# Weight conversion in bits, a batch turned by TensorE, and another order of pieces, in a linear-attention and mixer kernel

## The chip, the cores and the metric

The kernel runs on one core of a Trainium2 chip. The metric is the device time of one execution in microseconds (us). A profile of one execution gives, for every instruction, its engine, start and length; its span runs from the first to the last instruction.

## The reference

Inputs are `q`, `k`, `v`, `f_logit` of shape (4, 8, 768, 48) in float32, and the float64 weights `U` (768 x 32), `V` (32 x 768), `w_ch1` (384 x 1536) and `w_ch2` (1536 x 384).

```python
f = 1.0 / (1.0 + np.exp(-f_logit))
for t in range(S):
    state = f[:, :, t, :, None] * state + np.einsum('bhd,bhe->bhde', k[:, :, t], v[:, :, t])
    y[:, :, t] = np.einsum('bhd,bhde->bhe', q[:, :, t], state)
x = y.transpose(0, 2, 1, 3).reshape(B, S, H * D)
u = x + (x.transpose(0, 2, 1) @ U @ V).transpose(0, 2, 1)
out = u + np.maximum(u @ w_ch1, 0.0) @ w_ch2
```

## The kernel before

A unit is two heads of one batch (16 units, four a batch), with 2 x 48 head dimensions padded to 2 x 64 partitions and the 768 steps in six chunks of 128.

`prepare(n)` readies a unit. SyncE has loaded f, k and q into `f_raw`, `k_raw`, `q_raw` (two sets) so that VectorE can turn them (dimension to partition) by one transpose of 32 x 32 blocks each (`turned`, L237). `gates` makes the sigmoid on ScalarE (L255, L257), `keep` a backward scan X on VectorE (L261) with four small instructions, `keys` turns k, which GpSimd multiplies by X (L276), `read` is the forward scan Y (L280), `queries` turns q, which GpSimd multiplies by Y (L285), and issues the loads of unit n + 2.

`attend(n)` uses it: `scores` (two halves) multiplies k and q on TensorE (`sc`, L308) and VectorE masks the result (`A`, L315); `kept` turns k back on TensorE (`pt`, L327), copied by ScalarE (`kb`, L329); `states` makes the state changes (`ds`, L335) and adds them up on VectorE (`st`, L341, L346); `read` makes the outputs (`y`, L363 and L372), copied by ScalarE into the batch's `x` (L378).

The mixer of a batch is a list of pieces: `low_rank` (`ph`, L79, copied to `h`), six `mix` (`pu`, L86; VectorE adds it to x, L87), six `turn` (`put`, L95; copied to `uT`, L97), then for each half of the tokens twelve `ch1` (`pz`, L102; ScalarE's ReLU gives `z`, L105) and three `ch2` (`po`, L111; VectorE adds x, L114, SyncE stores). The pieces of the mixer of batch b are strewn in equal numbers among the pieces of the units of batch b + 1 by `fill`; the last mixer follows at the end.

The weights come in 32 pieces, strewn in the same way among batch 0's units. `load` fetches a piece into `w_raw` (two buffers; `V` takes four loads a piece) and converts float64 to float32 by six VectorE instructions (L49, L51, L53 to L56) and two GpSimd ones (L57, L58).

All loads and stores are issued by SyncE, in one order. A scheduler of the framework sorts the instructions into one fixed order for each engine when the program is built, starting from the order in which they are written; on the chip each engine goes through its own in that order, waiting on semaphores. The PSUM pools hold three large buffers (`ps_big`: `sc`, `pt`, `y`) and two small ones (`ps_mm`: all else). A second path for the case that X gets too small is built, and skipped at run time.

Of the kernel before, what the change touches and what calls it, by code (L numbers as in the profile page):

```python
# [8 lines left out]
F32 = mybir.dt.float32  # L9
# [12 lines left out]


def weight_loader(nc, pool, one, dma):

    P = nc.NUM_PARTITIONS  # L30

    def load(dst, w, copies=1):
        rows, cols = dst.shape
        n = rows // copies
        if w.dtype == F32:
            for i in range(copies):
                dma.dma_start(out=dst[i * n : (i + 1) * n, :], in_=w)
            return
        raw = pool.tile([P, WP], U64, name="w_raw")
        for i in range(copies):  # L40
            dma.dma_start(out=raw[i * n : (i + 1) * n, 0:cols], in_=w)
        words = raw[0:rows, 0:cols].bitcast(U32).rearrange("p (n two) -> p n two", two=2)
        lo, hi = words[:, :, 0], words[:, :, 1]

        def tmp(dtype, name):
            return one.tile([P, WP], dtype, name=name)[0:rows, 0:cols]

        head, m = tmp(U32, "w_head"), tmp(F32, "w_m")
        nc.vector.tensor_scalar(head, hi, 0xFFFFF, 0x100000, ALU.bitwise_and, ALU.bitwise_or)  # L49

        nc.vector.scalar_tensor_tensor(m, lo, 2.0**-32, head, ALU.mult, ALU.add)  # L51
        e, e8, s = tmp(U32, "w_e"), tmp(U32, "w_e8"), tmp(U32, "w_s")
        nc.vector.tensor_scalar(e, hi, 20, 0x7FF, ALU.logical_shift_right, ALU.bitwise_and)  # L53
        nc.vector.tensor_scalar(e8, e, 1023.0 - 127.0, 0.0, ALU.subtract, ALU.max)
        nc.vector.tensor_scalar(e, e8, 255.0, 2.0**23, ALU.min, ALU.mult)
        nc.vector.scalar_tensor_tensor(s, hi, 0x80000000, e, ALU.bitwise_and, ALU.bitwise_or)  # L56
        nc.gpsimd.tensor_scalar(m, m, 2.0**-20, None, ALU.mult)  # L57
        nc.gpsimd.tensor_tensor(dst, m, s.bitcast(F32), ALU.mult)  # L58

    return load  # L60


def mixer_pieces(nc, b, x, U, V, w1, w2, ident, out, two, three, zp, ps_mm):

# [64 lines left out]
def factored_path(ctx, tc, q, k, v, f_logit, moe_U, moe_V, moe_w_ch1, moe_w_ch2, out, ok):  # L129
# [257 lines left out]
    for piece in prepare(0):  # L387
        piece()
# [364 lines left out]
```

## Time and profile before

| | |
|---|---|
| time before, median of 3 runs | 663.54 us (661.59 to 666.61) |
| the profiled execution | 667.96 us, its span 666.2 us |
| busy in the span | TensorE 544.8 (82%), VectorE 326.5 (49%), GpSimd 127.3 (19%), ScalarE 96.8 (15%) |
| moved by the DMA queues | 48.44 MB in 42,471 packets |

In a profile's rows PE is TensorE's matmuls (PEld its weight loads, which run beside them), DVE VectorE, ACT ScalarE, POOL GpSimd and SP SyncE. A float32 product of 128 x 128 by 128 x 384 is two MATMUL instructions in the trace, and one in the order. `x24` counts instructions.

### The profile page before, as it was taken

The page shows a single profiled execution, that of the slowest core. Times are in us where ns is not written, and L with a number is a line of the kernel's source. Part 1 is how long each engine was busy: PE and PEld are TensorE (multiplying, and loading weights), DVE is VectorE, ACT ScalarE, POOL GpSimd, SP SyncE. Part 2 cuts the span into 40 slices and gives each one's busy share as a digit, 9 for nine tenths or more (in the row PEclk, how much of TensorE's full clock was granted, in tenths as well). Part 3 has the DMA queues.
Part 4 walks back from the last instruction along what each step waited for, and adds up shares of the span by engine and source line. Part 5 has one row for each costly group of instructions (what it writes and reads, how often), then busy time and mean ns, then how long its engine had stood idle before and what let it go on. Part 6 is the DMA issues. An engine that isn't in the chain of part 4 may idle for free.

```text
span 666.2 us, 8766 instructions
## 1 busy us (share of the span) xinstructions
PE 544.8 (82%) x3593; PEld 339.3 (51%) x3593; DVE 326.5 (49%) x534; ACT 96.8 (15%) x189; POOL 127.3 (19%) x107
## 2 busy tenths in 40 slices
PE   0555037277099999999999999999999998999996
PEld 0554034054066565646655556566556564555553
DVE  5669799999985674365642652473011102000000
ACT  1100001012021032021220220212101201210200
POOL 2123464655642201202111111021100000000000
PEclk9999999999579999996999999979999999999999
DMA  9901654544589050295002522210000000000000
GB/s 203 187 1 36 146 142 115 138 116 130 145 181 209 31 120 0 64 201 119 5 19 76 141 66 63 74 25 1 1 24 14 0 13 26 0 1 35 0 14 28
DMA packets 42471, 48.44 MB, mean 73 GB/s; under 512 B 29878, under 2 KB 32950, under 8 KB 42422
## 3 DMA queue, kind: packets, MB, share of 16 engines
q1 hardware_dynamic: 42422, 47.79, 29.7%
q8 instruction: 30, 0.49, 0.3%
q14 instruction: 19, 0.16, 0.1%
HBM read 43.06 MB, written 4.72 MB: 72 GB/s over the span
## 4 chain that ended last, share of the span: by engine, by line
PE 67%; DVE 18%; DMA 7%; issue 3%; SPq 2%; POOL 1%; ACT 1%; DVEq 0%; POOLq 0%; ACTq 0%
PE po L111 27%; PE pz L102 27%; PE sc L308 4%; PE y L372 3%; DVE w_m L51 2%; DVE kT L237 2%; DMA q_raw<-in_q_dram 2%; PE pu L86 2%; DMA w_raw<-in_moe_w_ch_dram 2%; DMA k_raw<-in_k_dram 2%; DVE fT L237 2%; SPq L179 1%; DVE qT L237 1%; DVE w_head L49 1%; DVE X L261 1%
## 5 line engine op out<-in xcount | busy, mean ns | idle before, releaser
L102 PE MATMUL pz<-uT,w 128*128 128x384 f32 x576 | 202.5, 505 | 1.2 <-ACT z L105 1.2
L111 PE MATMUL po<-w,z 128*128 128x384 f32 x576 | 189.2, 488 | 0.0
L102 PEld LDWEIGHTS pz<-uT,w 128*128 128x128 f32 x576 | 110.0, 196 | 74.4 <-issue 6.3
L111 PEld LDWEIGHTS po<-w,z 128*128 128x128 f32 x576 | 108.7, 190 | 74.7
L308 PE MATMUL sc<-qT,kT 48*128 48x128 f32 x384 | 42.7, 356 | 92.2 <-POOL qT L285 92.2
L114 DVE TENSOR_TENSOR o<-x,po 128x384 f32<-128x384 f32 x24 | 13.3, 556 | 182.7 <-PE po L111 182.7
L308 PEld LDWEIGHTS sc<-qT,kT 48*128 48x128 f32 x384 | 34.2, 246 | 105.6 <-POOL qT L285 94.4
L105 ACT ACTIVATE z<-pz 128x384 f32<-128x384 f32 x96 | 47.0, 490 | 223.3 <-PE pz L102 223.3
L276 POOL TENSOR_TENSOR kT<-kT,X 128x768 f32<-128x768 f32 x16 | 29.4, 1836 | 239.8 <-DVE kT L237 166.2
L315 DVE TENSOR_TENSOR A<-sc,causal 128x384 f32<-128x384 f32 x64 | 33.2, 551 | 73.0 <-PE sc L308 72.9
L57 POOL TENSOR_SCALAR w_m<-w_m 128x384 f32<-128x384 f32 (+1 forms) x32 | 34.1, 1065 | 34.3 <-DVE w_m L51 25.6
L237 DVE STREAM_TRANSPOSE fT<-f_raw 128x768 f32<-128x768 f32 x16 | 33.3, 2079 | 9.8 <-DMA f_raw<-in_f_logit_dram 9.8
L285 POOL TENSOR_TENSOR qT<-qT,Y 128x768 f32<-128x768 f32 x16 | 29.2, 1827 | 45.9 <-DVE qT L237 40.4
L237 DVE STREAM_TRANSPOSE qT<-q_raw 128x768 f32<-128x768 f32 x16 | 33.6, 2099 | 6.6 <-PE y L363 6.6
L261 DVE TENSOR_TENSOR_SCAN X<-fz,ends 128x768 f32<-128x768 f32 x16 | 28.4, 1775 | 15.9 <-ACT f L257 10.9
L237 DVE STREAM_TRANSPOSE kT<-k_raw 128x768 f32<-128x768 f32 x16 | 33.1, 2071 | 0.0
L372 PE MATMUL y<-v_nat,A 128*64 128x48 f32 x768 | 32.1, 252 | 0.0
L363 PE MATMUL y<-st,qT 48*64 48x48 f32 x640 | 20.7, 255 | 13.6 <-DVE st L346 8.6
L280 DVE TENSOR_TENSOR_SCAN Y<-fz,starts 128x768 f32<-128x768 f32 x16 | 28.1, 1755 | 6.3 <-POOL qT L285 5.5
L372 PEld LDWEIGHTS y<-v_nat,A 128*64 128x64 f32 x768 | 29.9, 167 | 1.1
L86 PE MATMUL pu<-h,V 128*128 128x384 f32 x48 | 25.0, 622 | 6.1 <-ACT h L82 2.5
L58 POOL TENSOR_TENSOR w<-w_m,w_s 128x384 f32<-128x384 f32 x24 | 26.1, 1087 | 16.1 <-DVE w_s L56 16.0
(49 smaller groups left out, 320.2 us busy)
## 6 DMA issues: line engine op xcount, KB each, us to landing
w_raw<-in_moe_w_ch_dram SPq DMA_DIRECT2D x24, 384.0 KB, 3.8
f_raw<-in_f_logit_dram SPq DMA_DIRECT2D x63, 142.0 KB, 4.9
k_raw<-in_k_dram SPq DMA_DIRECT2D x63, 142.0 KB, 4.2
q_raw<-in_q_dram SPq DMA_DIRECT2D x63, 142.0 KB, 4.6
v_nat<-in_v_dram SPq DMA_DIRECT2D x32, 144.0 KB, 5.4
out_dram<-o SPq DMA_DIRECT2D x24, 192.0 KB, 1.9
w_raw<-in_moe_V_dram SPq DMA_DIRECT2D x8, 96.0 KB, 2.2
w_raw<-in_moe_U_dram SPq DMA_DIRECT2D x6, 32.0 KB, 1.8
```

The lines of the kernel that those rows point to most:

```text
L57: nc.gpsimd.tensor_scalar(m, m, 2.0**-20, None, ALU.mult)
L86: nc.tensor.matmul(pm[:, 0:DM], lhsT=V[:, t * P : (t + 1) * P], rhs=h[0], start=True, stop=True)
L102: nc.tensor.matmul(pm[:, 0:HALF], lhsT=w1[:, m, i * P : (i + 1) * P], rhs=uT[a][:, m, :], start=(m == 0), stop=(m == NDC - 1))
L105: nc.scalar.activation(z[a, i], pm[:, 0:HALF], AF.Relu)
L111: nc.tensor.matmul(pm[:, 0:DM], lhsT=z[a, i][:, s * P : (s + 1) * P], rhs=w2[:, i, :], start=(i == 0), stop=(i == NFC - 1))
L237: nc.vector.transpose(t.rearrange("p (i c) -> p c i", c=TB), bass.AP(src_tile.tensor, src_tile.offset, [list(src_tile.ap[0]), [D, TB], [1, ...
L261: nc.vector.tensor_tensor_scan(backwards(X, S - 1, S), backwards(f, S, S), backwards(ends, S - 1, S), 0.0, ALU.mult, ALU.add,)
L276: nc.gpsimd.tensor_tensor(kT, kT, T["X"], ALU.mult)
L285: nc.gpsimd.tensor_tensor(qT, qT, T["Y"], ALU.mult)
L308: nc.tensor.matmul(sc[:, par, c * C : (c + 1) * C], lhsT=T["k"][rows[par], chunk[g * G + c]], rhs=T["q"][rows[par], chunk[g * G + c]], sta ...
L315: nc.vector.tensor_tensor(T["A"][:, par, g * G : (g + 1) * G, :], sc[:, par, 0 : G * C].rearrange("p (c i) -> p c i", i=C), causal.unsquee ...
L372: nc.tensor.matmul(o(a, par, c), lhsT=T["A"][:, par, c, halves[a]], rhs=vt[:, c, par, :], start=False, stop=True, skip_group_check=True,)
```

## The change

1. A weight piece takes two ScalarE instructions (L57, L58), three VectorE ones (L59 to L61) and one integer addition on GpSimd (L62). `w_raw` has three buffers, and a piece's load is issued two pieces ahead of its conversion (`ahead_by`). `U` is one piece and each piece of `V` one load: 27 pieces.
2. f, k and q of batch 0 are loaded as they lie in memory, in runs of 192 bytes, turned by TensorE (`on_tensor`, six transposes each) and taken from PSUM by ScalarE: f by the sigmoid, k and q by a copy.
3. `w_ch2` is converted among the first pieces of the first mixer, in batch 1's units, no longer in batch 0's. `Fill` strews by a cost that each piece carries.
4. The pieces of a unit and of the next unit's preparation stand in another order, with `kept` ahead of the scores.
5. The three `ch2` of a mixer's second half stand after the next batch's attention, around `low_rank` and `mix` of the next mixer.
6. The sigmoid's table is loaded at the start.

TensorE's queue at the start. `sc`, `pt`, `ds` and `y` are as above; in the new order `pt` with `f_raw`, `k_raw`, `q_raw` are the six transposes of an operand. Before:

```order
L308 MATMUL sc<-qT,kT 128x128 x6
L327 MATMUL pt<-ident,kT 128x64 x10
L308 MATMUL sc<-qT,kT 128x128 x6
L335 MATMUL ds<-v_nat,kb 64x48 x10
L363 MATMUL y<-st,qT 64x48 x20
```

After:

```order
L321 MATMUL pt<-ident,f_raw_80 128x128 x6
L321 MATMUL pt<-ident,k_raw_81 128x128 x6
L321 MATMUL pt<-ident,q_raw_82 128x128 x6
L321 MATMUL pt<-ident,f_raw_83 128x128 x6
L418 MATMUL pt<-ident,kT 128x64 x10
L321 MATMUL pt<-ident,k_raw_84 128x128 x6
L399 MATMUL sc<-qT,kT 128x128 x6
L426 MATMUL ds<-v_nat,kb 64x48 x10
L321 MATMUL pt<-ident,q_raw_85 128x128 x6
L399 MATMUL sc<-qT,kT 128x128 x6
L454 MATMUL y<-st,qT 64x48 x20
```

Eighteen transposes of a unit went into TensorE's queue, the next unit's among this unit's products.

VectorE's queue where batch 1 begins, with its first unit's k (`k_raw_81`) turned and the first mixer's `pu` added to x. Before (`w_head`, `w_e`, `w_m`, `w_s` are steps of a weight piece):

```order
L87 TENSOR_TENSOR x<-x,pu 128x384
L56 SCALAR_TENSOR_TENSOR w_s<-w_raw,w_e 128x384
L87 TENSOR_TENSOR x<-x,pu 128x384
L49 TENSOR_SCALAR w_head<-w_raw 128x384
L53 TENSOR_SCALAR w_e<-w_raw 128x384
L51 SCALAR_TENSOR_TENSOR w_m<-w_raw,w_head 128x384
L54 TENSOR_SCALAR w_e_576<-w_e 128x384
L87 TENSOR_TENSOR x<-x,pu 128x384
L55 TENSOR_SCALAR w_e<-w_e_576 128x384
L237 STREAM_TRANSPOSE kT<-k_raw_81 128x24x32
```

After (`w_y` are a piece's steps):

```order
L132 TENSOR_TENSOR x<-x,pu 128x384 x4
L302 STREAM_TRANSPOSE kT<-k_raw_81 128x24x32
L132 TENSOR_TENSOR x<-x,pu 128x384
L302 STREAM_TRANSPOSE qT<-q_raw_82 128x24x32
L406 TENSOR_TENSOR A<-sc,causal 128x384
L59 TENSOR_SCALAR w_y<-w_y 128x384
L406 TENSOR_TENSOR A<-sc,causal 128x384
L60 TENSOR_SCALAR w_y<-w_y 128x384
```

The pieces, which stood among the additions to x, now stand behind that unit's first masks. Nine of the 27 stand ahead of this place, 18 behind it, the last of them after the transpose of f of the last unit of batch 1.

TensorE's queue where batch 1 ends. Before:

```order
L111 MATMUL po<-w_122,z 128x384 x24
L308 MATMUL sc<-qT,kT 128x128 x6
L79 MATMUL ph<-x,U 32x384 x6
L327 MATMUL pt<-ident,kT 128x64 x9
L86 MATMUL pu<-h,V 128x384 x2
```

After:

```order
L156 MATMUL po<-w_124,z 128x384 x12
L124 MATMUL ph<-x,U 32x384 x6
L156 MATMUL po<-w_124,z 128x384 x12
L131 MATMUL pu<-h,V 128x384
L418 MATMUL pt<-ident,kT 128x64 x2
L131 MATMUL pu<-h,V 128x384 x2
L418 MATMUL pt<-ident,kT 128x64 x2
```

The `po` of the last mixer's second half moved to both sides of `ph`.

The diff, cut; lines taken out of `load` stand in the kernel above, and the second path takes the same loader.

```diff
-def weight_loader(nc, pool, one, dma):
+SMALLEST = struct.unpack("f", struct.pack("I", 896 << 20))[0]
+LARGEST = struct.unpack("f", struct.pack("I", (1151 << 20) - 2))[0]
+def weight_loader(nc, pool, dma):
     P = nc.NUM_PARTITIONS
-    def load(dst, w, copies=1):
-        rows, cols = dst.shape
-        n = rows // copies
+    def load(dst, w):
         if w.dtype == F32:
...
+            return lambda: dma.dma_start(out=dst, in_=w), lambda: None
+        rows, n = dst.shape[0], dst.free_size()
+        flat = dst if len(dst.shape) == 2 else dst.rearrange("p c n -> p (c n)")
+        T = {}
+        def start():
+            raw = T["raw"] = pool.tile([P, WP], U64, name="w_raw", bufs=3)[0:rows, 0:n]
+            if len(dst.shape) == 3:
+                raw = raw.rearrange("p (c n) -> p c n", c=dst.shape[1])
+            dma.dma_start(out=raw, in_=w)
+        def end():
+            y = pool.tile([P, WP], U32, name="w_y")[0:rows, 0:n]
+            r = pool.tile([P, WP], I32, name="w_r")[0:rows, 0:n]
+            words = T["raw"].bitcast(U32).rearrange("p (n two) -> p n two", two=2)
+            lo, hi = words[:, :, 0], words[:, :, 1]
+            f = y.bitcast(F32)
+            nc.scalar.activation(f, hi.bitcast(F32), AF.Abs)
+            nc.scalar.activation(r, lo, AF.Copy, scale=2.0**-29)
+            nc.vector.tensor_scalar(f, f, SMALLEST, LARGEST, ALU.max, ALU.min)
+            nc.vector.tensor_scalar(y, y, 3, 0x3FFFFFFF, ALU.logical_shift_left, ALU.bitwise_and)
+            nc.vector.scalar_tensor_tensor(y, hi, 0xC0000000, y, ALU.bitwise_and, ALU.bitwise_or)
+            nc.gpsimd.tensor_tensor(flat.bitcast(I32), y.bitcast(I32), r, ALU.add)
+        return start, end
...
+def ahead_by(n, loads):
+    for start, _ in loads[:n]:
+        start()
+    def call(i):
+        if i + n < len(loads):
+            loads[i + n][0]()
+        loads[i][1]()
+    return [lambda i=i: call(i) for i in range(len(loads))]
+class Fill:
+    def __init__(self, pieces, portions):
+        self.pieces = list(pieces)
+        self.share = sum(c for c, _ in self.pieces) / portions
+        self.due = 0.0
+    def __call__(self):
+        self.due += self.share
+        while self.pieces and self.pieces[0][0] / 2 <= self.due:
+            cost, piece = self.pieces.pop(0)
+            self.due -= cost
+            piece()
+    def rest(self):
+        while self.pieces:
+            self.pieces.pop(0)[1]()
...
-    todo = [low_rank]
-    for t in range(NCH):
-        todo.append(lambda t=t: mix(t))
-        if t:
-            todo.append(lambda t=t: turn(t - 1))
-    todo.append(lambda: turn(NCH - 1))
+    before = [(DM, low_rank)]
+    before += [(2 * DM, lambda t=t: mix(t)) for t in range(NCH)]
+    before += [(DM, lambda t=t: turn(t)) for t in range(NCH)]
+    main = []
     for a in range(2):
-        todo += [lambda a=a, i=i: ch1(a, i) for i in range(NFC)]
-        todo += [lambda a=a, s=s: ch2(a, s) for s in range(TPH)]
-    return todo
+        main += [(2 * NDC * HALF, lambda a=a, i=i: ch1(a, i)) for i in range(NFC)]
+        if a == 0:
+            main += [(2 * NFC * DM, lambda s=s: ch2(0, s)) for s in range(TPH)]
+    after = [(2 * NFC * DM, lambda s=s: ch2(1, s)) for s in range(TPH)]
+    return before, main, after
...
+    nat = [
+        {nm: t[:, 0 : NCH * 2 * PAD].rearrange("p (c h d) -> p c h d", h=2, d=PAD) for nm, t in slot.items()}
+        for slot in raw
+    ]
+    for slot in nat:
+        for nm, t in slot.items():
+            nc.gpsimd.memset(t[:, :, :, D:PAD], 20.0 if nm == "f" else 0.0)
     src = {"f": f_logit, "q": q, "k": k, "v": v}
     v_tiles = {}
     def load_unit(n):
         b, hp = divmod(n, HP)
         for nm in "fkq":
+            if b == 0:
+                for par in range(2):
+                    nc.sync.dma_start(
+                        out=nat[n % 2][nm][:, :, par, 0:D],
+                        in_=src[nm][b, 2 * hp + par].rearrange("(c p) d -> p c d", p=C),
+                    )
+                continue
...
+    load = weight_loader(nc, two, nc.sync)
+    weights = [load(U, moe_U.rearrange("(c p) r -> p c r", p=P))]
+    weights += [load(V[:, o : o + WP], copies(moe_V, P // R, o, WP)) for o in range(0, S, WP)]
     weights += [
-        lambda o=o, c=c: load(w1[:, c, o : o + WP], moe_w_ch1[c * P : (c + 1) * P, o : o + WP])
+        load(w1[:, c, o : o + WP], moe_w_ch1[c * P : (c + 1) * P, o : o + WP])
         for o in range(0, FF, WP)
         for c in range(NDC)
     ]
-    weights += [lambda i=i: load(w2[:, i, :], moe_w_ch2[i * P : (i + 1) * P, :]) for i in range(NFC)]
+    first = len(weights)
+    weights += [load(w2[:, i, :], moe_w_ch2[i * P : (i + 1) * P, :]) for i in range(NFC)]
...
+        def on_tensor(nm):
+            pt = ps_big.tile([P, 2, 512], F32, name="pt", tag="big")
+            for c in range(NCH):
+                nc.tensor.transpose(
+                    pt[:, c // G, c % G * C : (c % G + 1) * C],
+                    nat[n % 2][nm][:, c].rearrange("p h d -> p (h d)"), ident,
+                )
+            return pt[:, :, 0 : G * C].rearrange("p a (c t) -> p a c t", t=C)
+        def halves(t):
+            return t[:, 0:S].rearrange("p (a c t) -> p a c t", a=2, t=C)
+        def operand(nm, of):
+            t = T[nm] = two.tile([P, S], F32, name=f"{nm}T")
+            if b == 0:
+                nc.scalar.copy(halves(t), on_tensor(nm))
+            else:
+                turned(t, r[nm])
+            nc.gpsimd.tensor_tensor(t, t, T[of], ALU.mult)
         def gates():
+            f0 = T["f0"] = two.tile([P, NCH], F32, name="f0")
+            if b == 0:
+                pt = on_tensor("f")
+                nc.scalar.activation(halves(f)[:, :, :, 1:C], pt[:, :, :, 1:C], AF.Sigmoid)
+                nc.scalar.activation(f0.rearrange("p (a c) -> p a c", a=2), pt[:, :, :, 0], AF.Sigmoid)
+                return
...
-        return [lambda: scores(0), kept, lambda: scores(1), states, read]
+        return [kept, lambda: scores(0), states, lambda: scores(1), read]
     load_unit(1)
+    loads = ahead_by(2, weights)
+    todo = [(1, f) for f in loads[:first]]
     for piece in prepare(0):
         piece()
-    todo = list(weights)
+    after = []
     for b in range(B):
-        left = [HP * 10]
-        def fill():
-            m = -(-len(todo) // left[0])
-            left[0] -= 1
-            for _ in range(m):
-                todo.pop(0)()
-        for hp in range(HP):
-            n = b * HP + hp
-            work = attend(n)
-            ahead = prepare(n + 1) if n + 1 < NU else []
-            for i, piece in enumerate(work):
+        fill = Fill(todo, HP * 10)
+        for n in range(b * HP, (b + 1) * HP):
+            kept, scores, states, scores2, read = attend(n)
+            if n + 1 < NU:
+                gates, keep, keys, read_back, queries = prepare(n + 1)
+                order = [gates, kept, keep, keys, scores, states, read_back, queries, scores2, read]
+            else:
+                order = [kept, scores, states, scores2, read]
+            for piece in order:
+                fill()
                 piece()
-                fill()
-                if i < len(ahead):
-                    ahead[i]()
-                fill()
-        assert not todo
-        todo = mixer_pieces(nc, b, x_tiles[b], U, V, w1, w2, ident, out, two, three, zp, ps_mm)
+        fill.rest()
+        before, main, last = mixer(b)
+        if b == 0:
+            todo = before + main[0:NFC]
+            for i, f in enumerate(loads[first:]):
+                todo.insert(2 * i + 1, (0, f))
+            todo += main[NFC:]
+        else:
+            after[1:1] = before[0:1]
+            after[3:3] = before[1 : 1 + NCH]
+            after += before[1 + NCH :]
+            for _, piece in after:
+                piece()
+            todo = main
+        after = last
...
-    for f in todo:
-        f()
+    for _, piece in todo + after:
+        piece()
```

More of the change, by code (lines that the diff above doesn't have):

```diff
@@ L273, in keys @@
         def keys():
[L274 to L276 removed]
+            operand("k", "X")
         def read():
@@ L291, in factored_path, with mixer @@
     x_tiles = {}
+    def mixer(b):
+        return mixer_pieces(nc, b, x_tiles[b], U, V, w1, w2, ident, out, two, three, zp, ps_mm)
     def attend(n):
@@ L677, in general_path @@
     FILLS = NL + 3
[L678 removed]
     for n in range(NSLOT):
         load_unit(n)
+    todo = [(1, f) for f in ahead_by(2, weights)]
     for b in range(B):
[L682 to L688 removed]
+        fill = Fill(todo, HP * FILLS)
         for hp in range(HP):
             attention(b * HP + hp, fill)
[L692 to L694 removed]
+        fill.rest()
+        todo = [p for part in mixer(b) for p in part]
+    for _, f in todo:
         f()
```

61 lines of the change are left out of this document (12 added, 49 removed).

## The prediction

> **What bounds the kernel now.** I read the page first (shares of the engines, the forty slices, the chain of waits), then cut the run where the chain changes hands.
>
> ```profile
> PE   0555037277099999999999999999999998999996
> DVE  5669799999985674365642652473011102000000
> PE 67%; DVE 18%; DMA 7%; issue 3%; SPq 2%; POOL 1%; ACT 1%; DVEq 0%; POOLq 0%; ACTq 0%
> ```
>
> VectorE is full for a quarter of the run and TensorE from there to the end. I cut at the first low-rank product `ph` (104.64), where TensorE becomes full (197), and at the `ph` of the third and fourth mixer. The view of stretches has time: each engine's busy us, granted clock, DMA share, GB/s.
>
> ```profile
> 0.00:104.64 104.64, 38.03 (x569) 34.34 (x569) 80.64 (x153) 11.21 (x19) 37.54 (x44) 1.00 0.54 121
> 104.64:197.00 92.36, 51.08 (x374) 31.02 (x374) 87.78 (x158) 10.24 (x20) 53.49 (x44) 0.87 0.52 135
> 197.00:424.40 227.40, 223.36 (x1442) 135.81 (x1442) 117.29 (x151) 40.00 (x80) 29.01 (x16) 0.98 0.37 87
> 424.40:556.70 132.30, 130.32 (x887) 78.98 (x887) 33.88 (x61) 20.21 (x39) 7.23 (x4) 0.97 0.05 16
> 556.70:666.20 109.50, 101.98 (x330) 59.13 (x330) 6.87 (x14) 15.11 (x31) 0.00 (x0) 1.00 0.04 14
> ```
>
> Stage 1 (attention of batch 0) has VectorE busy 81 of 105, stage 2 (weights, first units of batch 1) 88 of 92. After 197 TensorE is 98% busy. So VectorE's work counts before 197 only; after it, only TensorE's own gaps count. The chain gives TensorE's prices at full speed and its gaps:
>
> ```profile
> 442.09 1.58 PE sc L308 x10
> 443.66 5.90 PE pz L102 x12
> ...
> 450.02 4.07 PE pz L102 x12
> ...
> 522.53 0.87 PE sc L308 x12
> ...
> 527.46 0.72 PE ds L335 x20
> ...
> 538.05 0.73 PE y L363 x40
> 538.78 1.53 PE y L372 x48
> ...
> 556.73 1.50 PE ph L79 x12
> ...
> 567.77 23.22 PE pz L102 x72
> ```
>
> Half a mixer product is 23.22, so one mixer's four halves are 92.9. An attention unit is 2 x 0.87 + 0.72 + 0.73 + 1.53 + about 0.5 for `kept` (10 instructions where `ds` has 20, and its start) = 5.2. The chain `ph`, `pu`, `put` in the clear takes 567.77 - 556.73 = 11.0; its TensorE work is 1.5 + 3.9 (12 `pu` instructions at 23.22/72) + about 2 for the transposes = 7.4.
>
> **Stage 1, step by step.** VectorE loses 12 of these 48 block transposes, 12 x 98.31/48 = 24.6, and the six-step conversion of 32 weight pieces: 66.4 for the instructions that read `w_raw`, and L54 and L55 at 9.7 and 11.0. The first two rows are the view of stretches for these instructions alone (the whole run, VectorE's busy time), the others the groups of instructions by shape, with the mean ns of one behind the bar:
>
> ```profile
> 0.00:666.20 666.20, 98.31 (x48) 0.97 0.30 73
> 0.00:666.20 666.20, 66.39 (x128) 0.97 0.30 73
> ...
> L54 DVE TENSOR_SCALAR w_e<-w_e 128x384 uint32<-128x384 uint32 x26 | 9.7, 374 | 0.0
> L55 DVE TENSOR_SCALAR w_e<-w_e 128x384 uint32<-128x384 uint32 x26 | 11.0, 422 | 0.3
> L56 DVE SCALAR_TENSOR_TENSOR w_s<-w_raw,w_e 128x384 uint32<-128x384 uint32 x26 | 14.6, 563 | 0.5
> L49 DVE TENSOR_SCALAR w_head<-w_raw 128x384 uint32<-128x384 uint32 x26 | 14.7, 567 | 3.2 <-DMA w_raw<-in_moe_w_ch_dram 3.1
> L58 POOL TENSOR_TENSOR w<-w_m,w_s 128x384 f32<-128x384 f32 x24 | 26.1, 1087 | 16.1 <-DVE w_s L56 16.0
> L97 ACT COPY uT<-put 128x384 f32<-128x384 f32 x24 | 11.5, 479 | 38.3 <-PE put L95 38.3
> L255 ACT ACTIVATE fz<-fT 128x762 f32<-128x762 f32 x16 | 13.4, 838 | 84.5 <-DVE fT L237 74.4 <-DVE st L346 10.1
> L261 DVE TENSOR_TENSOR_SCAN X<-fz,ends 128x768 f32<-128x768 f32 x16 | 28.4, 1775 | 15.9 <-ACT f L257 10.9 <-ACT fz L255 4.6
> L280 DVE TENSOR_TENSOR_SCAN Y<-fz,starts 128x768 f32<-128x768 f32 x16 | 28.1, 1755 | 6.3 <-POOL qT L285 5.5
> L315 DVE TENSOR_TENSOR A<-sc,causal 128x384 f32<-128x384 f32 x64 | 33.2, 551 | 73.0 <-PE sc L308 72.9
> L346 DVE SCALAR_TENSOR_TENSOR st<-st,whole 128x48 f32<-128x48 f32 x64 | 21.7, 338 | 1.6
> ```
>
> A piece now costs VectorE three instructions, like L54, L55 and L56: 0.37 + 0.42 + 0.56 = 1.36; ScalarE two, like L97: 0.96; GpSimd one, like L58: 1.09, where it paid two. 27 pieces: 36.7 in VectorE's queue, so it is freed of 24.6 + 87.1 - 36.7 = 75. The new forms are not in the trace; L54 and L49 (0.37 to 0.57) bound them on VectorE, and ScalarE's could cost L255's 0.84.
>
> What is late next? TensorE, which is slow here. The instructions in order of time (start, length, in brackets the idle time before):
>
> ```profile
> 5.37 2.08 DVE L237 STREAM_TRANSPOSE fT<-f_raw 128x768 f32<-128x768 f32 x1 [3.38 <-DMA f_raw<-in_f_logit_dram]
> ...
> 19.64 1.65 PE L308 MATMUL sc<-qT,kT 48*128 48x128 f32 x12 [19.64 <-POOL qT L285]
> ...
> 23.15 1.31 PE L335 MATMUL ds<-v_nat,kb 128*64 128x48 f32 x20
> ...
> 24.96 1.07 PE L363 MATMUL y<-st,qT 48*64 48x48 f32 x24 [0.51 <-DVE st L341]
> 27.60 0.77 PE L363 MATMUL y<-st,qT 48*64 48x48 f32 x16 [1.57 <-DVE st L346]
> 28.30 2.80 PE L372 MATMUL y<-v_nat,A 128*64 128x48 f32 x48
> ...
> 111.74 0.90 PE L95 MATMUL put<-ident,x 128*128 128x128 f32 x3 [0.82 <-DVE x L87]
> ```
>
> Twelve `sc` take 1.65, not 0.87, though the granted clock reads 1.00: half speed. So 18 transposes are about 18 x 0.23 = 4.1 (0.90 for three, with 0.2 of start), and a unit of attention 2 x 1.65 + 0.75 (`kept` by the same measure) + 1.31 + 1.07 + 0.77 + 2.80 = 10.0: 14.1 a unit. VectorE's chain beside it (sigmoid 1.04 with its short second part, X 1.78, small ones 0.6, Y 1.76, four masks 2.2, five states 1.7, then `y`) comes to the same 14. f lands at 5.4 at the latest. TensorE's queue up to the first `y` is six operands, `kept`, two `sc` and `ds`, 6 x 1.4 + 0.75 + 3.3 + 1.3 = 13.8; with masks 1.1 and `y` 4.6 that is 25, and 28 with the waits for two units' scans and loads, my estimate. Three more rounds, the last without its 4.1 of transposes, give 28 + 42.3 - 4.1 = **66** for stage 1 instead of 104.6. At full speed the round is about 11 and the stage 59.
>
> The natural loads are 192-byte packets in place of 4,544-byte ones, with half the bytes. The stretch of such `v` loads against one of the long rows:
>
> ```profile
> 12.50:18.50 6.00, 0.00 (x0) 0.00 (x0) 5.21 (x3) 0.00 (x0) 2.54 (x2) 1.00 1.03 225
> 28.50:30.40 1.90, 1.90 (x40) 1.90 (x40) 1.82 (x2) 0.04 (x1) 0.00 (x0) 1.00 1.46 227
> ```
>
> 225 against 227 GB/s: a unit's eight DMAs, 1.18 MB, take 5.2 us, less than a round, so I charge nothing. The Trainium skill ("DMA: Bandwidth & Descriptors", Specifications) speaks against this step: below 512 bytes a transfer loses line rate. This trace's stretch does not agree; were the rate halved, a unit would take 10.4, and beside the weights' loads the stage would become DMA's (second rival).
>
> **Stage 2.** By the order, nine weight pieces are converted in stage 1 and 18 in stage 2, and TensorE's first `po` needs the last twelve. VectorE's queue up to the last one: 10 transposes 20.5, four X and three Y 12.4, small ones 3, six additions to x priced like masks 3.3, masks and states of two units 8, 18 x 1.36 = 24.5: 72. It also stands still: the first mask of unit 4 is queued ahead of the weights and waits for a `sc` that TensorE has queued behind the whole chain and seven `pz` (about 8 us), the next units' masks 4 more; and the last eight pieces are paced by three `w_raw` buffers:
>
> ```profile
> w_raw<-in_moe_w_ch_dram SPq DMA_DIRECT2D x24, 384.0 KB, 3.8
> ```
>
> (3.8 + 0.48 + 1.36)/3 = 1.9 a piece, 0.5 over VectorE's price, 4 in all. Stage 2: 72 + 16 = **88**, against 92.4. Bounds: 65, TensorE's own work there plus the chain's waits, and 105, if SyncE, which queues the next units' loads behind weight loads that wait for a buffer, makes each of three units 6 late. But TensorE does far more in it: chain 7.4, `ch1` 23.2, units 4 and 5 and part of 6 12.6, 22 `po` pairs 14.2: 57. Of batch 1 (7.4 + 3 x 23.2 + 4 x 5.2 = 98) **41** are left.
>
> **The later batches.** 424.4 to 556.7 takes 132.3. The new order puts `ch2` of the last mixer around the chain: its 11.0 - 7.4 = 3.6 of waiting goes. With it goes, I take, the slow spell behind it (`sc` x10 at 1.58 for 0.73, `pz` x12 at 5.90 for 4.07, `y` alike: 3.3). 125.4 each, **250.8** for two. VectorE's own work, 34 busy here and some 60 where transposes are among it, lies beside it. The last: 109.5 + 23.2 (moved here) - 2.6 = **130.1**, its last 5.5 the final addition and store.
>
> **Sum.** 66 + 88 + 41 + 250.8 + 130.1 = 575.9; the profiled execution is 1.76 longer than its span (667.96 against 666.2): 577.7. That execution stands 0.7% above the median of 663.54, so 577.7 x 663.54/667.96 = **574**.
>
> **Rivals.** (1) TensorE goes to full speed in stage 1, being busy nearly without a break, and carries it into stage 2: 59, and 72 for stage 2 (the chain 9 shorter, fewer buffer waits 7): 554.7, or 551. For it: from 197 on, under dense work, it runs at full speed. Against: between 19.64 and 28.30 it stood at most 1.6 us at a time and `y` was still at 2.80. The Trainium skill ("TensorE: Matmul & The Clock Gate", Part 1) promises full clock after some 3.4 us of activity, which would make this the likeliest; the rows just named don't agree.
>
> (2) Loads bind: small packets at half rate and SyncE blocked behind weight buffers: stage 1 at 80, stage 2 at 105: 608.7, or 605. For it: DMA share 0.54 and 0.52 already. Against: 227 GB/s.
>
> (3) Slower: each piece's two ScalarE instructions wait for its load, with sigmoids, `kb` and `z` copies queued behind. If all 27 pieces lay open, 27 x (3.8 + 0.96) = 129: 706, or 702. It ends above the old time once 70% of that reaches TensorE (the whole gain is 90). Against: VectorE, which had the same place in the queue, waited 3.1 us in all for `w_raw` (L49). A part of it, or freed VectorE time that TensorE cannot use, gives no change.
>
> **Chances.** Forecast with its neighbourhood, 558 to 592: 0.55. Rival 1: 0.22. Rival 2: 0.16. No change: 0.03. Slower: 0.04. About 1% is what can be told from none. The range goes from below rival 1 (with stage 2 at its bound of 65: 544) to rival 2: 543 to 605.
>
> **What would show it.** Right: first `ph` near 66, 12 `sc` at 1.65 before it; `po` waiting on the weights for some 20 us before 154; about 125 between later `ph`s; no `pz` group of 12 near 5.9 behind a chain. Wrong: ScalarE's idle time ended by `w_raw` loads, `w` instructions above 0.6, SyncE waiting on buffers while transposes wait for f, a later `ph` distance of 130.

## The result, and the profile after

The changed kernel takes 610.32 us (median of 4 runs, 609.27 to 610.99) against 665.08 us (661.59 to 667.79): a ratio of 0.918 with a 95% interval of 0.913 to 0.923. Forecast were 574, in a range of 543 to 605: the kernel became faster, as forecast, but by 55 us where 90 were expected, and its time lies above the range. The profiled execution has a span of 607.5 us, where the prediction's sum came to 575.9: 31.6 us are to be found.

The page, first the slices of the engines and of the DMA queues, then the shares of the chain of waits:

```profile
PE   4876889767689999999999999999999999999995
DVE  5799738777845655154845633145122020000000
DMA  9884608814869210502455122010000000000000
...
PE 77%; DVE 11%; DMA 6%; ACT 2%; issue 2%; POOL 1%; SPq 0%; DVEq 0%; POOLq 0%; ACTq 0%
```

TensorE is full from the thirteenth slice on, at 182 us, and before it was from the twelfth of its longer slices, at 183; but it has far more behind it by then, and its share of the chain rose from 67 to 77%. In slices 8 to 11 (106 to 167 us) TensorE is six to seven tenths busy and VectorE seven to eight, and the DMA queues fall silent in slice 6 and nearly so in slice 9. The view of stretches, cut at the prediction's places: first `ph`, last weight piece, second, third and fourth `ph`, end. Columns: length, busy time of TensorE, its weight loads, VectorE, ScalarE and GpSimd, granted clock, DMA share, GB/s.

```profile
0.00:66.46 66.46, 45.11 (x640) 37.97 (x641) 53.68 (x91) 24.21 (x45) 29.20 (x34) 0.80 0.85 156
66.46:169.73 103.27, 76.81 (x476) 42.56 (x476) 72.69 (x115) 33.23 (x68) 30.18 (x24) 0.81 0.50 127
169.73:221.69 51.96, 51.91 (x375) 31.58 (x375) 26.20 (x35) 9.51 (x19) 7.30 (x4) 0.96 0.58 130
221.69:352.96 131.27, 130.15 (x900) 78.91 (x899) 70.84 (x92) 24.57 (x49) 19.68 (x10) 0.99 0.30 74
352.96:481.99 129.03, 128.18 (x899) 78.24 (x898) 34.45 (x62) 20.99 (x41) 7.26 (x4) 1.00 0.08 24
481.99:607.50 125.51, 117.77 (x380) 67.89 (x379) 8.74 (x17) 14.94 (x31) 0.00 (x0) 0.98 0.04 15
```

Against the prediction's terms:

| stretch | forecast | measured | difference |
|---|---|---|---|
| stage 1 | 66 | 66.5 | +0.5 |
| stage 2 | 88 | 103.3 | +15.3 |
| rest of batch 1 | 41 | 52.0, of it 7.9 for a `po` group that now stands ahead of the second `ph` | +3.0 without that group |
| two batches | 250.8 | 260.3 | +9.5 |
| last part | 130.1 | 125.5, and the 7.9 of that group | +3.3 |

Half of what is missing lies in stage 2. What VectorE waited for there (view of waits, this stretch alone: us, times, longest):

```profile
DVE A L406 <- PE sc L399: 13.0, 5, 10.7
DVE w_y L59 <- ACT w_y L57: 6.0, 6, 2.2
DVE X L353 <- ACT fz L348: 3.9, 4, 1.6
DVE st L432 <- PE ds L426: 3.7, 1, 3.7
DVE x L132 <- PE pu L131: 2.7, 2, 2.1
```

VectorE was busy for 72.7 of the 103.3 us, and 72 had been forecast; it stood for 30.6, where 16 had been forecast. TensorE's instructions at the end of that stage, in order of time (start, length, in brackets the idle time before), and the boundary of the table above:

```profile
138.18 0.80 PE L418 MATMUL pt<-ident,kT 64*128 64x64 f32 x10 [6.74 <-POOL kT L336]
...
160.18 1.56 PE L156 MATMUL po<-w,z 128*128 128x384 f32 x4 [0.40 <-POOL w L62]
162.54 1.56 PE L156 MATMUL po<-w,z 128*128 128x384 f32 x4 [0.80 <-POOL w L62]
169.78 11.07 PE L156 MATMUL po<-w,z 128*128 128x384 f32 x28 [5.68 <-POOL w L62]
...
213.75 8.01 PE L156 MATMUL po<-w,z 128*128 128x384 f32 x24
221.69 1.49 PE L124 MATMUL ph<-x,U 128*32 128x384 f32 x12
```

`po` waits for the weights piece by piece until 169.8, not until 154. Ahead of that TensorE stood 6.7 us because the preparation of batch 1's third unit came late.

### The profile page after: what moved, and what is told of

Read it like the earlier page. It is cut to its first block, busy times and chain, and to the rows that moved or that the text cites. A ratio compares the mean times of both kernels' runs of the same rounds, so it can differ in the third digit from the quotient of the medians.

```text
span 607.5 us, 8789 instructions
## 1 busy us (share of the span) xinstructions
PE 549.9 (91%) x3665; PEld 337.1 (55%) x3665; DVE 266.6 (44%) x411; ACT 127.5 (21%) x252; POOL 93.6 (15%) x76
## 4 chain that ended last, share of the span: by engine, by line
PE 77%; DVE 11%; DMA 6%; ACT 2%; issue 2%; POOL 1%; SPq 0%; DVEq 0%; POOLq 0%; ACTq 0%
PE pz L147 30%; PE po L156 30%; PE y L463 4%; PE sc L399 4%; PE pu L131 3%; DMA w_raw<-in_moe_w_ch_dram 2%; DMA k_raw<-in_k_dram 2%; PE y L454 2%; DVE Y L370 2%; DVE X L353 2%; PE put L140 1%; PE ds L426 1%; DVE A L406 1%; PE ph L124 1%; DVE fT L302 1%
## 5 line engine op out<-in xcount | busy, mean ns | idle before, releaser
L156 PE MATMUL po<-w,z 128*128 128x384 f32 x576 | 198.1, 500 | 10.2 <-POOL w L62 10.2
L159 DVE TENSOR_TENSOR o<-x,po 128x384 f32<-128x384 f32 x24 | 13.3, 554 | 192.2 <-PE po L156 192.2
L399 PE MATMUL sc<-qT,kT 48*128 48x128 f32 x384 | 39.1, 310 | 5.3 <-POOL qT L336 5.3
L353 DVE TENSOR_TENSOR_SCAN X<-fz,ends 128x768 f32<-128x768 f32 x16 | 28.6, 1788 | 32.2 <-ACT f L349 10.9
L399 PEld LDWEIGHTS sc<-qT,kT 48*128 48x128 f32 x384 | 29.7, 202 | 21.0 <-issue 13.6
L336 POOL TENSOR_TENSOR qT<-qT,Y 128x768 f32<-128x768 f32 x16 | 31.8, 1988 | 37.1 <-DVE X L360 15.6
L370 DVE TENSOR_TENSOR_SCAN Y<-fz,starts 128x768 f32<-128x768 f32 x16 | 29.5, 1841 | 7.5 <-POOL qT L336 6.8
L62 POOL TENSOR_TENSOR w<-w_y,w_r 128x384 int32<-128x384 int32 x24 | 25.3, 1052 | 46.3 <-DVE w_y L61 41.8
L454 PE MATMUL y<-st,qT 48*64 48x48 f32 x640 | 18.4, 240 | 12.5 <-DVE st L432 6.8
L454 PEld LDWEIGHTS y<-st,qT 48*64 48x64 f32 x640 | 14.3, 143 | 21.5 <-DVE st L437 8.0
L302 DVE STREAM_TRANSPOSE fT<-f_raw 128x768 f32<-128x768 f32 x12 | 25.0, 2080 | 0.4 <-DMA f_raw<-in_f_logit_dram 0.3
L302 DVE STREAM_TRANSPOSE qT<-q_raw 128x768 f32<-128x768 f32 x12 | 25.1, 2088 | 0.0
L302 DVE STREAM_TRANSPOSE kT<-k_raw 128x768 f32<-128x768 f32 x12 | 24.9, 2073 | 0.0
L131 PE MATMUL pu<-h,V 128*128 128x384 f32 x48 | 21.3, 560 | 1.6 <-DVE x L132 1.1
```

The costliest lines, as they stand in the source:

```text
L131: nc.tensor.matmul(pm[:, 0:DM], lhsT=V[:, t * P : (t + 1) * P], rhs=h[0], start=True, stop=True)
L156: nc.tensor.matmul(pm[:, 0:DM], lhsT=z[a, i][:, s * P : (s + 1) * P], rhs=w2[:, i, :], start=(i == 0), stop=(i == NFC - 1))
L302: nc.vector.transpose(t.rearrange("p (i c) -> p c i", c=TB), bass.AP(src_tile.tensor, src_tile.offset, [list(src_tile.ap[0]), [D, TB], [1, ...
L336: nc.gpsimd.tensor_tensor(t, t, T[of], ALU.mult)
L353: nc.vector.tensor_tensor_scan(backwards(X, S - 1, S), backwards(f, S, S), backwards(ends, S - 1, S), 0.0, ALU.mult, ALU.add,)
L370: nc.vector.tensor_tensor_scan(Y, f[:, 0:S], e, 0.0, ALU.mult, ALU.add)
```

## The theories

The silences of the DMA queues gave the first theory. The view of waits of the whole run, SyncE's queue:

```profile
SPq L48 <- DVE w_y L61: 79.2, 17, 27.7
```

SyncE stood 79 us at loads of weights that had no free `w_raw`, the next units' loads queued behind: for 28 us from 65.7 on, and again from 121.3 to 141.6. **Buffers**: this lengthens stage 2. **Order**: the pieces stand behind masks, copies and preparations in the fixed order of VectorE and ScalarE, and SyncE's wait only mirrors that. **Pace**: a piece is dearer than its instructions, through GpSimd and the two `w_y` buffers.

## Experiments

All twelve runs beside the kernel before on the same chip (ratio with 95% interval); `ph` from the profiled executions.

| run | us | ratio | first `ph` | from there to the second |
|---|---|---|---|---|
| the changed kernel | 610.3 | 0.918 (0.913 to 0.923) | 66.5 | 155.2 |
| raw5 | 598.1 | 0.898 (0.893 to 0.903) | 70.5 | 145.7 |
| wq_act | 612.2 | 0.920 (0.914 to 0.926) | 91.5 | 136.2 |
| now2 | 580.6 | 0.871 (0.866 to 0.876) | 68.2 | 130.8 |
| nolow | 601.9 | 0.904 (0.899 to 0.910) | 65.8 | 151.7 |
| w2early | 586.7 | 0.879 (0.877 to 0.881) | 69.7 | 132.1 |
| turnv | 633.9 | 0.950 (0.948 to 0.952) | 95.6 | 153.0 |
| ch2in | 619.4 | 0.927 (0.924 to 0.930) | 68.0 | 171.7, all three `po` groups ahead of the second `ph` |
| bigpk | 608.1 | 0.910 (0.909 to 0.912) | 77.3 | 144.6 |
| early5 | 593.6 | 0.890 (0.887 to 0.894) | 80.2 | 129.4 |
| earlypool | 609.7 | 0.916 (0.912 to 0.920) | 111.7 | 112.9 |
| oldconv | 634.1 | 0.951 (0.946 to 0.956) | 82.9 | 165.4 |
| early_y3 | 585.4 | 0.877 (0.874 to 0.880) | 70.8 | 130.1 |

### More buffers: raw5

```diff
-raw = ... pool.tile([P, WP], U64, name="w_raw", bufs=3)
+raw = ... pool.tile([P, WP], U64, name="w_raw", bufs=5)
-loads = ahead_by(2, weights)
+loads = ahead_by(4, weights)
```

> The changed kernel with five w_raw buffers in place of three, and each weight load issued four pieces ahead in place of two. Theory BUFFERS (SyncE's loads stand behind weight loads that wait for a buffer: the DMA queues moved nothing from 65 to 94 and from 121 to 141 us): the silences shrink, the unit loads come earlier, and the second stage (first ph to the last w2 piece) falls from 103 to about 90: 595 to 600 us. Theory ORDER (the weight pieces stand behind masks and kb copies in the fixed order of VectorE and ScalarE, and SyncE's wait is only the mirror of that): SyncE waits less, but the stage stays within 3 us: 607 to 612. Theory PACE (a piece takes 1.95 us because GpSimd's addition holds up the next piece and w_y has two buffers): no change, 608 to 612.

598.1 us: the time that Buffers gave, but not by its way. SyncE's wait and stage 2 of this run:

```profile
SPq L48 <- DVE w_y L61: 78.4, 14, 24.3
```

```profile
70.45:164.94 94.49, 73.39 (x474) 41.44 (x474) 64.95 (x102) 30.39 (x62) 26.85 (x22) 0.85 0.40 100
```

SyncE waits as long as before, and VectorE stands 94.5 - 65.0 = 29.5 us as before. What fell is VectorE's work in the stage, 72.7 to 65.0: 11 pieces instead of 9 are converted ahead of the first `ph`, since the order put them there, and three scans X and three Y lie in the stage instead of four of each. So the place of the pieces counts. Some 5 us more came later: the two middle batches took 127.8 and 128.0.

That SyncE's wait stayed as long does not by itself speak against Buffers. The lead grew with the buffers: the load of piece i + 4 waits for the buffer of piece i - 1, as the load of piece i + 2 did, and five buffers with the old lead were not tried. What speaks against Buffers is the changed kernel's own view of waits: in stage 2 no engine waited for a load of f, k or q, and the loads of weights held up ScalarE's conversions alone, four times and for 4.6 us in all. The chain of waits does run through loads in parts of this stretch, for the longest time until 114.1; but there ScalarE went from its copy of `kb` (113.56) to the next conversion (114.15) without idle time.

### Another queue for the weights: wq_act

```diff
-load = weight_loader(nc, two, nc.sync)
+load = weight_loader(nc, two, nc.scalar)
```

> The changed kernel with the weight loads issued by ScalarE, and all other loads by SyncE as before, so that no unit load stands behind a weight load. BUFFERS: 595 to 600 us, less what ScalarE loses by waiting for buffers itself (up to 5 us). ORDER and PACE: the unit loads land early, but the second stage keeps its 103 us or grows, as ScalarE now stands where SyncE stood: 608 to 620.

612.2: no unit load stands behind a weight load in SyncE's order now, and nothing is gained. The first `ph` moves out by 25 us, with 15 pieces ahead of it instead of 9, and presumably because ScalarE, which also takes the operands of batch 0 from PSUM, now waits for buffers itself; after it 19 us are won back. The range of Order and Pace holds it; Buffers' does not. But the run does not isolate the queue: SyncE's unit loads still waited 58.0 us in the whole run that the view of waits puts down to weight loads (`SPq L240 <- DMA w_raw`).

### Without `w_ch2`: now2

```diff
-weights += [load(w2[:, i, :], moe_w_ch2[...]) for i in range(NFC)]
+weights += [(lambda: None, lambda i=i: nc.gpsimd.memset(w2[:, i, :], 0.01)) for i in range(NFC)]
```

> The changed kernel without the loads and the conversion of w_ch2: each of its twelve pieces is one small GpSimd memset instead, so the output is not the reference's. What is left of the second stage's idle time then has nothing to do with w_ch2. All theories: TensorE's idle 26 us between the first ph and 170 us fall. BUFFERS and PACE: to under 8, 585 to 590 us. ORDER: the waits for the masks of units 4 to 6 behind their own sc and ds (about 15 us of VectorE's 31 idle) stay, 592 to 598.

580.6 us, and 130.8 from the first to the second `ph` instead of 155.2. So 30 us hang on `w_ch2`. The masks' waits outlast it, as Order said: from the first `ph` to 128.8 VectorE still waits 14.1 us for `sc`, 11.0 of them at once. But with no weights queued behind them they cost little: TensorE stands 8.5 us between the two `ph` instead of 26.5, and Order's 592 to 598, which charged these waits, was too high. What costs is not the waits alone but the pieces that stand behind them. The middle batches take 128.2 and 128.0 without idle time on TensorE:

```profile
198.99:327.23 128.24, 128.24 (x900) 78.15 (x899) 76.92 (x99) 25.18 (x51) 19.43 (x10) 1.00 0.31 74
327.23:455.24 128.01, 128.01 (x900) 78.24 (x899) 34.53 (x61) 20.87 (x41) 7.25 (x4) 1.00 0.09 26
```

### `w_ch2` early again: w2early

```diff
-todo = [(1, f) for f in loads[:first]]
+todo = [(1, f) for f in loads]
...
-for i, f in enumerate(loads[first:]):
-    todo.insert(2 * i + 1, (0, f))
```

> The changed kernel with the twelve pieces of w_ch2 back among batch 0's units, as before the change (all 27 pieces strewn there, none in batch 1). Without w_ch2 altogether the kernel took 580.6 us, so the price of converting it early is what this run has above that. Theory VECTOR: VectorE's 12 x 1.64 = 20 us more in the first stage, of which its 13 us of idle time there takes some: first ph near 76 to 80, then 131 to the second ph as without w_ch2: 590 to 594 us. Theory LOADS (DMA share 0.85 before the first ph): 4.7 MB more at the 156 GB/s of that stage are 30 us: first ph near 95, or pieces that slip into the second stage again: 605 to 612.

586.7 us: 23.6 less than the changed kernel, and 6 more than without `w_ch2` at all. Stages 1 and 2 (to the last piece), and VectorE's waits in stage 2:

```profile
0.00:69.67 69.67, 51.59 (x640) 43.71 (x640) 57.12 (x102) 28.36 (x53) 33.02 (x38) 0.70 0.83 160
69.67:139.55 69.88, 61.22 (x420) 35.08 (x420) 50.05 (x85) 25.68 (x54) 22.80 (x19) 0.86 0.58 150
```

```profile
DVE w_y L59 <- ACT w_y L57: 9.5, 4, 5.7
DVE A L406 <- PE sc L399: 6.4, 4, 2.4
DVE x L132 <- PE pu L131: 3.5, 2, 3.3
```

The view of groups for stage 2 has 14 pieces here and 18 in the changed kernel; the first row is w2early's, the second the changed kernel's:

```profile
L61 DVE SCALAR_TENSOR_TENSOR w_y<-w_raw,w_y 128x384 uint32<-128x384 uint32 x14 | 8.4, 602 | 0.2
```

```profile
L61 DVE SCALAR_TENSOR_TENSOR w_y<-w_raw,w_y 128x384 uint32<-128x384 uint32 x18 | 11.9, 660 | 0.4
```

Only four pieces moved into stage 1, for 3.2 us there. Yet stage 2 lost 22.6 us of VectorE's work (72.7 to 50.1) and 10.8 of its idle time (30.6 to 19.8): the last pieces no longer stand behind the preparation of a further unit (two scans X lie in the stage instead of four, two transposes of k and of q instead of three). The cost was not the conversion of `w_ch2` as such but its place behind three units' work in VectorE's queue. SyncE still stands 64.7 us at the weight loads of this kernel, against 79.2, so a long wait of that queue and a short stage go together. The theory Loads, which had the first `ph` near 95, falls.

### How far it can be driven: early5, earlypool, early_y3

early5 has w2early's and raw5's edits together; earlypool moreover gives the weight loads to GpSimd (`nc.gpsimd` for `nc.sync`); early_y3 is w2early with this:

```diff
-y = pool.tile([P, WP], U32, name="w_y")
+y = pool.tile([P, WP], U32, name="w_y", bufs=3)
```

> Both: w_ch2 back among batch 0's units, and five w_raw buffers with loads four pieces ahead. In the order 16 pieces stand ahead of the first addition to x (9 in the changed kernel, 14 with w_ch2 early alone, 11 with five buffers alone). If the place of the pieces is what costs, each piece moved ahead is worth about 2 us in the second stage and costs under 1 in the first: 581 to 585 us. If the first stage's loads are at their limit (DMA share 0.92 with five buffers), the first ph moves out by as much as the second stage gains: 586 to 590.

> As the last, with the weight loads issued by GpSimd instead of SyncE: in the order all 27 pieces stand ahead of the first addition to x, and no unit load stands behind a weight load. The second stage then has no weights at all: 131 us from the first ph to the second. The first stage carries all loads, 15 MB or so: at 199 GB/s 75 us, at 156 GB/s 95 us. So 585 us if loads go at the better rate, 605 if at the worse, and more if GpSimd's issuing holds up its multiplications.

> The kernel with w_ch2 early (586.7 us), and three w_y buffers instead of two. A piece's first ScalarE instruction waits until GpSimd's addition of the piece two back has freed w_y; with that wait gone a piece in a row of pieces falls from 1.95 to about 1.6 us. If pieces in a row bind anywhere on the way to the second ph: 582 to 585 us. If not: 586 to 588.

early5 has 16 pieces ahead of the first `ph`, three more than w2early. They cost 10.5 us there (69.7 to 80.2) and bring 2.7 after it: 593.6, slower than w2early, and above both forecasts. earlypool has nearly all of them ahead: 112.9 from the first to the second `ph`, but the first only at 111.7, which gives 609.7, above its worse case of 605. Its loads went near the better rate, at 189 GB/s, but the first stage moved 111.68 x 189 = 21 MB and not the 15 expected. Stage 1 of both:

```profile
0.00:80.17 80.17, 53.46 (x640) 45.41 (x640) 65.87 (x112) 30.64 (x59) 37.78 (x41) 0.67 0.83 185
```

```profile
0.00:111.68 111.68, 64.05 (x668) 52.02 (x668) 93.57 (x154) 44.05 (x84) 66.12 (x80) 0.57 0.85 189
```

A first stage with more pieces is paid for in the first stage, and of the places tried w2early's is the best. early_y3 is 1.3 us below w2early, but the intervals of the two ratios overlap: whether the third `w_y` helps stays open. Both beat the changed kernel by about 4%.

### The price of a piece: nolow and oldconv

nolow drops the second ScalarE instruction and GpSimd's addition, and VectorE's third instruction writes the weight. oldconv brings back the old `load` body (six VectorE and two GpSimd instructions).

```diff
-nc.scalar.activation(r, lo, AF.Copy, scale=2.0**-29)
-nc.vector.scalar_tensor_tensor(y, hi, 0xC0000000, y, ...)
-nc.gpsimd.tensor_tensor(flat.bitcast(I32), y.bitcast(I32), r, ALU.add)
+nc.vector.scalar_tensor_tensor(flat.bitcast(U32), hi, 0xC0000000, y, ...)
```

> The changed kernel without the low words of the weights: no second ScalarE instruction and no GpSimd addition, VectorE's third instruction writes the weight itself. It leaves out the last three bits of each weight. PACE: a piece falls from 1.95 to about 1.3 us, 12 us less VectorE and GpSimd in the second stage, 593 to 598 us. BUFFERS and ORDER: the last eight pieces gain 5 us, nothing else moves: 602 to 606.

> The changed kernel with the old conversion of a weight piece: six VectorE and two GpSimd instructions, no ScalarE ones; everything else as changed. By the prediction's term VectorE gets 87.1 - 36.7 = 50 us more work; by the measured 1.64 a piece it is 43. Nine pieces lie in the first stage and 18 in the second. If VectorE sets the end of both stages, nearly all of it shows: 645 to 655 us. If the waits of the second stage (VectorE idle 31 of 103 us) hide a part: 630 to 640.

nolow: 601.9, at the lower end of what Buffers and Order gave (602 to 606) and outside Pace's 593 to 598: the price of a piece is only a small part. Of the 8.4 us 0.7 come in stage 1, 3.5 up to the second `ph`, the rest behind it. oldconv: 634.1, not 645 to 655. Its stage 2:

```profile
82.94:195.53 112.59, 79.01 (x476) 42.84 (x476) 98.15 (x163) 15.00 (x30) 55.52 (x42) 0.83 0.40 105
```

VectorE has 98.2 us of work there instead of 72.7, but stands for 14.4 instead of 30.6. Of the 25.5 us of VectorE's work that the new conversion saves in stage 2, 16 came back as VectorE's waiting: 112.6 became 103.3. In stage 1 16.5 us were gained.

### The other parts: turnv, ch2in, bigpk

turnv sets `b == 0` to false in `load_unit`, `operand` and `gates`, and leaves out the filling of the padding; ch2in puts all six `ch2` into `main` and leaves `after` empty; bigpk reads six neighbouring time steps of a head into one partition, with the padding filled to match:

```diff
-out=nat[n % 2][nm][:, :, par, 0:D], in_=src[nm][...].rearrange("(c p) d -> p c d", p=C)
+out=raw[n % 2][nm][:, par * NCH * PAD : par * NCH * PAD + NCH * D], in_=src[nm][...].rearrange("(p c) d -> p (c d)", p=C)
```

> The changed kernel with batch 0 loaded in long rows and turned by VectorE, as before the change; all else stays. By the prediction's term VectorE gets 12 x 2.05 = 24.6 us back in the first stage: first ph near 90, 630 us. Rival LOADS: the first stage is near the limit of its DMA share of 0.85 because of the 192-byte packets, and long rows at twice the bytes do it no harm, so that some of the 24.6 us is won back: first ph near 80, 618 us.

> The changed kernel with the three ch2 of a mixer's second half strewn with the rest of the mixer again, none of them around the next low_rank. By the prediction's step the new place gained 3.6 + 3.3 us in each of three chains: 628 us, later ph distances 132. By the traces (132.3 and 0.9 for a sc that stood outside, against 131.3 and 129.0) it gained 2 to 4 in each of the later batches and more at the last chain, which stands in the clear again: 615 to 620 us.

> The changed kernel with batch 0's f, k and q loaded in the same number of bytes but as 1152-byte runs, so that the time steps lie in a wrong order and the output is not the reference's. LOADS: the first stage's DMA share falls from 0.85 to about 0.6, more weight pieces come through before the first ph, the second stage is shorter: 595 to 600 us. If the 192-byte packets cost nothing, as the prediction charged: 606 to 610.

turnv: 633.9; turning on TensorE is worth 23.6 us (term: 24.6), though the first `ph` moved by 29.1, and some 5 us came back behind it. bigpk: 608.1, within 0.4%. With packets six times as long the DMA share of the first stage falls from 0.85 to 0.59, as Loads had it, but no time is gained: the first `ph` comes 10.9 us later, with the same nine pieces ahead of it, and the second where it was (222.0 for 221.7). ch2in: 619.4. Its stretches between the later `ph`s, and the last:

```profile
239.78:375.19 135.41, 130.14 (x899) 78.92 (x899) 64.77 (x88) 25.22 (x52) 17.63 (x8) 0.97 0.29 76
375.19:507.33 132.14, 128.03 (x887) 78.47 (x887) 39.29 (x66) 20.00 (x39) 12.42 (x6) 0.99 0.08 22
507.33:616.90 109.57, 102.63 (x332) 58.83 (x331) 7.62 (x15) 15.10 (x31) 0.00 (x0) 1.00 0.04 14
```

The new place gained 4.1 and 3.1 us in the two middle batches, all of it idle time of TensorE (5.3 and 4.1 us in ch2in, 1.1 and 0.9 in the changed kernel); busy time is the same within 0.2.

## Why the prediction was right, and where it was wrong

**Stage 1: the number right, half the reason.** 66.5 for 66. TensorE's `sc` and `y` of the second and third unit, in order of time:

```profile
19.89 0.94 PE L399 MATMUL sc<-qT,kT 48*128 48x128 f32 x12
...
26.44 1.31 PE L463 MATMUL y<-v_nat,A 128*64 128x48 f32 x20
...
30.51 0.94 PE L399 MATMUL sc<-qT,kT 48*128 48x128 f32 x12
32.90 0.94 PE L399 MATMUL sc<-qT,kT 48*128 48x128 f32 x12
39.48 2.80 PE L463 MATMUL y<-v_nat,A 128*64 128x48 f32 x48
```

A round takes 14.5 us for 14.1, from the end of `y` at 27.8 to its end at 42.3. But TensorE does not set it: it is busy 45 of 66 us, and stands at half clock in part only (`y` x48 at 2.80, but most `sc` x12 at 0.94 instead of 1.65). What makes the round as long as forecast is a chain through VectorE, whose instructions beside GpSimd's are longer than the prediction had them (last section). From the chain of waits of that round (start, length):

```profile
29.79 1.77 DVE X L353
31.83 1.70 DVE whole L363
33.73 1.76 DVE Y L370
39.55 2.73 PE y L463 x48
```

The prediction had set VectorE's chain beside TensorE's at the same 14, with 0.6 for all its small instructions, where `whole` alone takes 1.70, and took TensorE's for the one that binds; that the number came out is in part luck. Rival 1, full clock and 59 us, did not come.

That the natural loads cost the kernel nothing held (bigpk), but the stretch named for it, 12.5 to 18.5 of the kernel before, is not one of `v` loads alone: SyncE issued four loads of q in it (from 12.71) and four of f (from 16.60), all in long rows, and two of `v`. In its first 40 us the changed kernel moves 160 GB/s at a DMA share of 1.00, bigpk 186 at 0.75. So the small packets do take more of the DMA engines' time; TensorE's waits for them in stage 1 come to 6.2 us, 4.6 of them one wait for f. The 24.6 us for the transposes held in the sum (turnv).

**Stage 2: the step that failed.** The prediction took VectorE's 72 of work and 16 of standing still. The work came out at 72.7. Of the standing, "about 8" for the first mask of unit 4 was 10.7, "4 more" for the next masks 2.3, and "4 in all" for the pace of the pieces 6.0; the waits for the sigmoids (3.9), for `ds` (3.7) and for `pu` (2.7) had no price at all. Together that is 13.3 us more than priced; the rest of the 15.3 is 0.7 of work and 1.3 of idle time that the view does not list. The prediction saw the row that shows the place, with the pieces behind unit 4's masks, and followed the queue's work on through units 5 and 6; but of the waits in it, it priced only those for masks and for the pieces themselves. w2early shows what the place costs: 23.6 us. The 3.0 us of the rest of batch 1 were not followed up.

**The second rival's time, not its cause.** Stage 2 came near the 105 of "loads bind", with SyncE blocked as it said; its 80 for stage 1 did not come. bigpk shows that the small packets did not make it so, and the view of waits that the blocked queue made no unit late: all that waited for loads in stage 2 were ScalarE's conversions, 4.6 us. That is also the third rival's mechanism, in small. Its last clause, freed VectorE time that TensorE cannot use, is the one that bit: 16 us of it (oldconv).

**The later batches: mis-sized.** 125.4 each against 131.3 and 129.0. "3.6 of waiting goes" was read from the last chain, which stood in the clear, but taken off a stretch in which TensorE's idle time had been only 132.3 - 130.3 = 2.0 us; and 1.1 and 0.9 of idle time are left. Moreover that stretch held 84 of a batch's 96 `sc` instructions, 0.9 us less work. With both put right, 132.3 + 0.9 - 2.0 - 3.3 = 127.9, which is the 128.0 that now2 and raw5 reach without idle time. The slow spell of 3.3 did go: no `pz` x12 stands near 5.9 behind a chain. It is not the chain's own, though: ch2in stands 4.1 us in a chain and has no slow `pz` behind it (four `pu` take 2.60 there instead of 1.56), and the first middle batch of the changed kernel has one elsewhere, behind a wait for `st`. There a transpose of f stands in VectorE's queue amid a unit's states; VectorE's row, TensorE's, and the clock behind them:

```profile
288.20 2.09 DVE L302 STREAM_TRANSPOSE fT<-f_raw 128x768 f32<-128x768 f32 x1
```

```profile
290.38 0.33 PE L454 MATMUL y<-st,qT 48*64 48x48 f32 x8 [0.89 <-DVE st L437]
...
292.74 9.05 PE L156 MATMUL po<-w,z 128*128 128x384 f32 x22
```

```profile
292.00:302.00 10.00, 10.00 (x58) 5.90 (x56) 8.88 (x8) 0.64 (x1) 5.17 (x2) 0.83 0.30 66
```

22 instructions took 9.05 where 24 take 8.01. That this follows from the wait was not tried.

**The last part** was 3.3 longer: the prediction took 2.6 off for the chain, and ch2in shows no such gain there (67.8 + 109.6 against 52.0 + 125.5).

**The signs.** Of the signs of being right the first `ph` near 66 came, and no `pz` x12 near 5.9 behind a chain. Most `sc` x12 ahead of that `ph` did not take 1.65, `po` waited on the weights past 154, and the later distances were not near 125. Of the signs of being wrong three came: a later distance of 130, `w` instructions above 0.6 (L61, 0.66), ScalarE idle until `w_raw` loads. The fourth came by half: SyncE waited on buffers, but no transpose waited for f in stage 2.

## What to carry to other kernels

Work that is moved "just in time" takes a place in every engine's queue; price it by everything that stands ahead of its last piece there, unit by unit, not by its own duration. A long wait of a DMA queue may be only the mirror of that place: five buffers with a longer lead left the wait as it was and helped through the order they caused. Ask first whether an engine waited for a load that the queue held back. And a wait may only be taken off the stretch that shows it as idle time.

## What the hardware did that was not expected

VectorE and GpSimd hold each other up. VectorE's row of pieces, and GpSimd's additions at the same time:

```profile
148.76 0.35 DVE L59 TENSOR_SCALAR w_y<-w_y 128x384 f32<-128x384 f32 x1
149.15 1.05 DVE L60 TENSOR_SCALAR w_y<-w_y 128x384 uint32<-128x384 uint32 x1
150.24 0.56 DVE L61 SCALAR_TENSOR_TENSOR w_y<-w_raw,w_y 128x384 uint32<-128x384 uint32 x1
```

```profile
148.99 0.99 POOL L62 TENSOR_TENSOR w<-w_y,w_r 128x384 int32<-128x384 int32 x1 [1.94 <-DVE w_y L61]
```

L60, which takes 0.36 alone, starts at 149.15 while the addition runs, and ends 0.2 us behind the addition's end. It goes the other way too: the last addition (167.42) takes 2.31 beside a scan of VectorE that runs to 168.94. In stage 1 the small `whole` takes 1.79 at 31.74, where GpSimd multiplies k from 31.69 to 33.50, and 0.16 in the kernel before. In nolow, without the additions, L60's like takes 0.36 throughout stage 2, against a mean of 0.51. The Trainium skill ("SBUF — State Buffer", Who interferes with whom) says that the one that comes second on the port pair these two engines share is blocked until the first has finished; these rows agree. With it a piece cost VectorE 1.67 in stage 2 (0.50 + 0.51 + 0.66), not 1.36: 18 x 0.31 = 5.6 us, which the prediction's 72 did not hold. It came out right all the same, by luck, because rows that follow each other overlap a little: the groups of that stretch add up to 78, the busy time to 72.7.
